# GpSimd's waits for VectorE's place in the order, left out of a gated-recurrence and maxout kernel

## Chip, cores and metric

The kernel runs on one core of a Trainium2 chip. The metric is the device time of one execution in microseconds; where a kernel was run several times, the median is given. A profiled execution is a run of its own with its own time, and the span in its profile goes from the first to the last instruction.

The engines are named as the profile names them: PE is TensorE (matmuls; PEld its weight loads), DVE is VectorE, ACT is ScalarE, POOL is GpSimd, SP is SyncE, which here issues all DMAs.

## What is computed

The inputs q, k, v and alpha have the shape batch 4, heads 8, sequence 768, head size 48. A gated linear recurrence keeps a 48x48 state for each batch and head, and its output goes as a token-by-feature matrix x (3072 x 384) through a maxout layer of two branches of width 1024:

```
for t in range(S):
    state = alpha[:, :, t, :, None] * state + einsum('bhd,bhe->bhde', k[:, :, t], v[:, :, t])
    y[:, :, t] = einsum('bhd,bhde->bhe', q[:, :, t], state)
x = y.transpose(0, 2, 1, 3).reshape(B * S, H * D)
out = maximum(x @ w1, x @ w2) @ w_out
```

## The kernel before

The sequence of each batch is cut into three blocks of 256 positions, which gives twelve blocks, n = 0 to 11. In a block, each of the 128 partitions holds two neighbouring positions, and the block is handled as two halves of 128 positions (64 partitions each). The recurrence in a block is written as matrix products: a masked product of scaled q and k within a half, and a carried state from one half to the next. The output of a block is cast into a transposed x (`xT`), and twelve groups g of two chunks of 128 tokens each run the maxout layer on it: with wd = w1 - w2, the layer is max(x@wd, 0) @ w_out + x @ (w2 @ w_out), so that one ReLU and one extra matrix m = w2 @ w_out do the work of the maximum.

Each piece of work is a named step. The steps of block n that matter here, with their line in the profile and the engines that they may run on:

- lda, ldk, ldq, ldv: loads of the block's inputs (SP, L448). ln, inv, en, ep, gg: logarithm of alpha and the exponentials (ACT).
- su{n} (L596, DVE or POOL): sum of the two positions' log alpha, both inputs in SBUF. cs{n} (L605, L610, PE): the running sums of it, by a matmul.
- ka{n} (L624) and qi{n} (L629), DVE or POOL: k and q scaled in place by the neighbour's alpha or its inverse. kt{n} (L661, DVE or POOL) and qt{n} (L666, DVE only, one input in PSUM): k and q scaled by the exponentials.
- tk, tq (L692, PE): transposes of the two; ck, cq (L490 on DVE, L488 on ACT): their copies out of PSUM. From block 8 on dk and dq (L732) do this by a DMA transpose instead.
- sc{n} (L832, PE) and pt{n} (L840, DVE, one input in PSUM): the masked product. vc{n}: cast of v. kv{n} (L752, PE): the block's own contribution to the state.
- g{n} (L765, POOL): a product of decays. With m = 2n or 2n+1 for the half, t32.m (L799) and T{m}.0, T{m}.1 (L787), on DVE or POOL: the carried state w{m-1} (L810, L812, DVE) scaled by the decay, once for the next state and twice, for the two head parities, as a matmul operand. yf{n} and y{n} (L877, PE): the block's output.
- xe (casts into xT: L488 on ACT, L490 on DVE), h{g} (L943, PE), r{g} (ReLU: L953 on ACT, L951 on DVE), o{g} (L976, PE), ev (eviction), st (store).
- at the start mask, pads, wtp, wtc, wd, woc, mp, mc prepare constants and weights, and 43 filler matmuls (L419) on a zero tile run on PE.

The number after a dot is the head half in blocks 0 and 1 (su0.0, su0.1), the head parity for T, and a part otherwise.

The order is not found at run time. `ORDER` is a string of words such as `su8.0:D`, step and engine (P PE, A ACT, D DVE, G POOL, S SP; a digit is a PSUM bank). `run()` returns the steps in that order and the loop at the end of the kernel emits them one by one; each engine then works through its own instructions in this order. Waits between engines follow from the tiles that a step reads and writes, and are added as the instructions are traced.

A step that is built with `port=True` is one that is marked as reading two inputs from SBUF, or as a copy within SBUF. The planner that once made the order (it does nothing while ORDER is there) did not start a POOL step while such a DVE step was under way, nor such a DVE step while POOL was at work. The loop carries a part of that into the program: after a marked step on DVE, the next step on POOL gets a wait for the end of that DVE step, whether or not it uses its data. There are 88 POOL steps in ORDER, and 22 of them get such a wait.

Of the kernel before, what the change touches and what calls it, by code (L numbers as in the profile page):

```python
# [299 lines left out]
def kernel(  # L300
# [15 lines left out]
    nc = tc.nc  # L316
# [687 lines left out]
        group(g, c0, nch)  # L1004
        c0 += nch

    traced = nc.cur_bb.bb.instructions
    ahead = None
    for o in plan.run():
        n = len(traced)  # L1010
        o.emit(o.eng)
        if o.eng == "DVE" and o.port:
            ahead = traced[-1]
        elif o.eng == "POOL" and ahead is not None:
            tc.add_manual_dep(traced[n], ahead.name,
                              mybir.DependencyInfo(mybir.DependencyClass.Sync, mybir.DependencyReason.DATA), reason="port")
            ahead = None
    Plan.last = plan


# [28 lines left out]
```

## Time and profile before

| | |
|---|---|
| median of 3 runs | 140.74 us (139.82 to 141.19) |
| the profiled execution's own time | 140.24 us |
| its span | 138.5 us |
| PE busy | 131.3 us, 95% of the span |
| DVE busy | 96.0 us, 69% |
| ACT busy | 79.8 us, 58% |
| POOL busy | 65.4 us, 47% |
| granted TensorE clock | 0.999 |

In lists of waits a line has the engine, the tile and line of the waiter, an arrow to the one that released it, and then the total time in us, how often, and the longest. In timelines a line has the start in us from the start of the span, the duration in us, the engine, the line of the kernel, the operation, and the tiles and shapes, output before input; x2 means two such instructions in a row, taken together. A duration in a timeline begins where the hardware records the start of an instruction, which can be before it gets to its data; waiting for a semaphore is not in it.

By its timeline POOL works on the steps of the first blocks until 21 us, pauses until 28 us, and then runs with gaps of up to 3 us until 111 us; a last T comes at 120 us.

### The profile page before, as it was taken

To read this page: it belongs to the slowest core of one execution; us is meant where nothing else is said; L and a number is where in the kernel's file an instruction comes from. 1 tells how busy PE (TensorE), PEld (TensorE's weight loads), DVE (VectorE), ACT (ScalarE), POOL (GpSimd) and SP (SyncE) were. 2 spreads that over 40 slices of the span, in tenths; PEclk is the share of its full clock that TensorE was granted. 3 is DMA by queue.
4 is the path that set the end of the run, shared out by engine and by line. 5 is a ranking of instruction groups with operands and counts; after the bars stand their busy time and mean duration, and the time that the engine had idled before them with its cause. 6 is when DMAs were issued, how large, how long until landed. Compare 5 with 4: busy or idle time off the path is not lost.

```text
span 138.5 us, 5457 instructions
## 1 busy us (share of the span) xinstructions
PE 131.3 (95%) x2348; PEld 94.0 (68%) x2348; DVE 96.0 (69%) x163; ACT 79.8 (58%) x163; POOL 65.4 (47%) x110
## 2 busy tenths in 40 slices
PE   6977999989999999999999999999999999999991
PEld 2445676655877686688866886776767876777770
DVE  5226769889877886798589759878975575685210
ACT  3526582869596779396883587543847732323320
POOL 6547360067568881796429499832625300100000
PEclk9999999999999999999999999999999999999999
DMA  4999999999999999999999991958998999541043
GB/s 108 266 304 304 380 385 326 217 249 273 267 248 226 275 262 255 282 271 278 253 274 303 280 282 29 139 98 175 287 168 215 140 199 162 193 172 60 0 170 114
DMA packets 64680, 30.76 MB, mean 222 GB/s; under 512 B 58896, under 2 KB 63120, under 8 KB 64656
## 3 DMA queue, kind: packets, MB, share of 16 engines
q1 hardware_dynamic: 64656, 30.41, 90.5%
q8 instruction: 18, 0.29, 1.0%
q14 instruction: 6, 0.05, 0.1%
HBM read 23.59 MB, written 4.72 MB: 204 GB/s over the span
## 4 chain that ended last, share of the span: by engine, by line
PE 70%; DMA 9%; SPq 9%; DVE 5%; POOL 2%; issue 2%; ACT 0%; DVEq 0%
PE PS L976 30%; PE PS L943 20%; DMA ldf<-in_k_dram 9%; PE PS L877 9%; SPq L448 6%; PE PS L832 4%; PE PS L692 4%; PE PS L752 2%; POOL ldf L629 2%; SPq L470 2%; DVE qkt L666 2%; SPq L467 1%; DVE qkt L661 1%; PE PS L605 1%; DVE pt L840 1%
## 5 line engine op out<-in xcount | busy, mean ns | idle before, releaser
L976 PE MATMUL PS<-wo,g 128*128 128x384 f16 (+1 forms) x200 | 37.6, 320 | 0.3 <-issue 0.3
L943 PE MATMUL PS<-xT,wd 128*128 128x256 f16 x288 | 36.2, 272 | 0.5 <-DVE xT L490 0.3
L840 DVE TENSOR_TENSOR pt<-PS,mask 128x1024 f16<-128x1024 f32 x24 | 28.9, 1218 | 4.2 <-PE PS L832 4.0
L943 PEld LDWEIGHTS <-wd 128*128 128x128 f16 x288 | 27.3, 98 | 5.8 <-issue 0.8
L953 ACT ACTIVATE g<-PS 128x512 f16<-128x512 f32 x34 | 19.6, 597 | 14.1 <-PE PS L943 13.9
L976 PEld LDWEIGHTS <-g 128*128 128x128 f16 x200 | 18.6, 98 | 11.2 <-issue 0.5
L629 POOL TENSOR_TENSOR ldf<-ldf,inv 128x384 f32<-128x384 f32 (+1 forms) x12 | 11.2, 933 | 17.5 <-DVE ldf L629 7.3
L488 ACT CAST xT<-PS 128x384 f16<-128x384 f32 x16 | 9.1, 595 | 15.1 <-PE PS L877 15.0
L976 PE MATMUL PS<-m,xT 128*128 128x384 f16 (+1 forms) x75 | 15.9, 320 | 0.0
L951 DVE TENSOR_SCALAR g<-PS 128x512 f16<-128x512 f32 x14 | 9.4, 684 | 7.2 <-PE PS L943 7.2
L419 PE MATMUL PS<-fz 128*128 128x512 f16 x43 | 12.9, 433 | 1.2 <-DVE fz L416 1.2
L666 DVE TENSOR_TENSOR qkt<-ldf,PS 128x768 f16<-128x768 f32 (+1 forms) x14 | 11.7, 835 | 3.2 <-POOL ldf L629 2.8
L787 POOL TENSOR_TENSOR T<-w,gg 48x192 f16<-48x192 f32 x15 | 7.8, 518 | 12.3 <-DVE T L787 3.2
L488 ACT COPY outs<-PS 128x384 f32<-128x384 f32 (+1 forms) x17 | 7.8, 460 | 9.0 <-PE PS L976 8.8
L661 POOL TENSOR_TENSOR qkt<-ldf,en 128x768 f16<-128x768 f32 (+1 forms) x7 | 11.9, 1702 | 2.0 <-ACT PS L644 1.8
L624 POOL TENSOR_TENSOR ldf<-ldf 128x384 f32<-128x384 f32 (+1 forms) x11 | 10.5, 962 | 3.4 <-DMA ldf<-in_k_dram 2.6
L588 ACT ACTIVATE loga<-ldf 128x768 f16<-128x768 f32 (+1 forms) x14 | 10.5, 751 | 2.3 <-DMA ldf<-in_alpha_dram 2.2
L787 POOL TENSOR_TENSOR T<-w,g 48x192 f16<-48x192 f32 x11 | 5.5, 503 | 12.7 <-DVE T L787 11.3
L692 PE MATMUL PS<-ident,qkt 128*128 128x128 f16 x128 | 10.3, 219 | 1.1 <-DVE qkt L666 0.9
L877 PE MATMUL PS<-pt,v 64*64 64x128 f16 x576 | 10.7, 218 | 0.0
L692 PEld LDWEIGHTS <-qkt 128*128 128x128 f16 x128 | 8.2, 98 | 3.1 <-DVE qkt L666 1.7
L490 DVE COPY qk<-PS 128x1024 f16<-128x1024 f16 (+1 forms) x12 | 7.2, 599 | 4.3 <-PE PS L692 4.1
(78 smaller groups left out, 187.4 us busy)
## 6 DMA issues: line engine op xcount, KB each, us to landing
ldf<-in_k_dram SPq DMA_DIRECT2D x12, 384.0 KB, 6.1
ldf<-in_q_dram SPq DMA_DIRECT2D x12, 384.0 KB, 6.3
ldf<-in_v_dram SPq DMA_DIRECT2D x12, 384.0 KB, 6.5
out_dram<-outs SPq DMA_DIRECT2D x23, 192.0 KB, 4.0
ldf<-in_alpha_dram SPq DMA_DIRECT2D x10, 384.0 KB, 6.0
ldf<-in_moe_w_dram SPq DMA_DIRECT2D x4, 768.0 KB, 8.2
ldf<-in_moe_w_out_dram SPq DMA_DIRECT2D x2, 768.0 KB, 9.7
ldf<-in_alpha_dram SPq DMA_DIRECT2D x4, 192.0 KB, 3.7
```

The lines of the kernel that those rows point to most:

```text
L419: plan.add(f"fill{i}", {"PE": 0.21}, lambda eng: nc.tensor.matmul(bank(fb), lhsT=fz[:, 0:128], rhs=fz, start=True, stop=True, skip_group_c ...
L488: nc.scalar.copy(out=out, in_=in_)
L629: e.tensor_mul(out=qq, in0=qq, in1=A["inv", n][:, hd])
L661: e.tensor_mul(out=hjd(qkts[i3], 1)[:, hd], in0=A["ld", n, "k"][:, hd].rearrange("p h (j d) -> p h j d", j=2), in1=f.unsqueeze(2).to_broad ...
L666: nc.vector.tensor_mul(out=hjd(qkts[i3], 0)[:, hd], in0=A["ld", n, "q"][:, hd].rearrange("p h (j d) -> p h j d", j=2), in1=f.unsqueeze(2). ...
L692: nc.tensor.transpose(t[:, a, r, j, :], src[:, j, r, :], ident16)
L787: e.tensor_mul(out=T16s[m % 4][o : o + 48, :, 48 * u : 48 * u + 48], in0=w_[o : o + 48], in1=g_[o : o + 48])
L840: nc.vector.tensor_mul(out=t.rearrange("p u r c -> p (u r) c"), in0=A["sc", n, hf].rearrange("p u (r c) -> p (u r) c", r=2), in1=mask.rear ...
L877: nc.tensor.matmul(dst, lhsT=lhsT, rhs=rhs, start=(x, u) not in begun, stop=done and ends[x, u] == i, skip_group_check=True)
L943: nc.tensor.matmul(t[:, i], lhsT=wd16[:, s, (f + i) * 128 : (f + i + 1) * 128], rhs=xT[:, s, a0 : a0 + W], start=(s == 0), stop=(s == 2), ...
L953: nc.scalar.activation(out=o, in_=i, func=ACTF.Relu)
L976: nc.tensor.matmul(A["op", t0, c], lhsT=lhsT, rhs=rhs, start=(part == 0 and j == 0), stop=(part == 1 and j + 1 == len(todo[1])))
```

## The change

After the change the loop emits the steps of `plan.run()` and does nothing else. The 22 waits that it had added are gone; the waits that follow from the tiles are still made. The steps, their engines, their order and their PSUM banks are the same, and each of the five engines has the same instructions in the same order as before. Where one of the added waits had also covered a wait for data on an earlier DVE or ACT step, that wait now stands by itself.

```
     for o in plan.run():
-        n = len(traced)
         o.emit(o.eng)
-        if o.eng == "DVE" and o.port:
-            ahead = traced[-1]
-        elif o.eng == "POOL" and ahead is not None:
-            tc.add_manual_dep(traced[n], ahead.name,
-                              mybir.DependencyInfo(mybir.DependencyClass.Sync, mybir.DependencyReason.DATA), reason="port")
-            ahead = None
     Plan.last = plan
```

The waits of these pairs go (POOL step after DVE step): su0.0 after su0.1, kt0.0 after ka0.0, qi0.0 after kt0.1, T1.0 after T1.1, g1 after woc0.1, qi1.1 after qi1.0, ka2.0 after su3.0, qi2.0 after kt2.0, qi3.0 after kt3.0, ka4.0 after su4.0, T9.0 after T9.1, ka6.0 after su5.0, T13.0 after t32.13, T10.1 after qi5.0, T11.0 after T10.0, qi9.0 after T15.0, ka8.0 after su8.0, T16.0 after T17.1, g10 after T19.0, t32.21 after su11.0, qi11.0 after kt11.0, T22.0 after T23.0.

More of the change, by code (lines that the diff above doesn't have):

```diff
@@ L1005 @@
         c0 += nch
-    traced = nc.cur_bb.bb.instructions
-    ahead = None
     for o in plan.run():
-        n = len(traced)
         o.emit(o.eng)
-        if o.eng == "DVE" and o.port:
-            ahead = traced[-1]
-        elif o.eng == "POOL" and ahead is not None:
-            tc.add_manual_dep(traced[n], ahead.name,
-                              mybir.DependencyInfo(mybir.DependencyClass.Sync, mybir.DependencyReason.DATA), reason="port")
-            ahead = None
     Plan.last = plan
```

## Prediction

> **What bounds the kernel now.** I read the busy shares first, then the waits of TensorE (PE), then those of GpSimd (POOL), and last the timelines of the places that the change touches. The page's first part:
>
> ```profile
> span 138.5 us, 5457 instructions
> PE 131.3 (95%) x2348; PEld 94.0 (68%) x2348; DVE 96.0 (69%) x163; ACT 79.8 (58%) x163; POOL 65.4 (47%) x110
> ```
>
> PE is busy 131.3 of 138.5 us, in an order that the change leaves alone. What PE still waits for is this, in full (engine, waiter, releaser: total us, times, longest):
>
> ```profile
> PE PS L419 <- DVE fz L416: 1.2, 1, 1.2
> PE PS L692 <- DVE qkt L666: 0.9, 2, 0.7
> PE PS L507 <- DMA ldf<-in_moe_w_dram: 0.7, 1, 0.7
> PE PS L943 <- DVE xT L490: 0.3, 1, 0.3
> ```
>
> Four smaller waits of 0.2 to 0.3 us follow. None names POOL. In PE's timeline the waits that are left after 13 us are some 1.3 us together: about 0.2 at 29.26 (tq1.1 for qt1.1), 0.2 at 30.23 (sc1.0 for cq1.1), 0.1 at 41.4 (kv2) and under 0.3 each at 47.9, 50.1 and 54.6. So PE's own work is the bound, and the change acts only through a wait of PE that it shortens or makes. POOL's waits are long but feed nothing late:
>
> ```profile
> POOL T L787 <- DVE T L787: 14.5, 3, 9.1
> POOL ldf L629 <- DVE ldf L629: 7.3, 1, 7.3
> POOL ldf L629 <- DVE qkt L661: 3.7, 2, 2.5
> POOL t L799 <- DVE s L596: 2.6, 1, 2.6
> ```
>
> Most of that idle time is the waits that go: the 9.1 us is T22.0 behind T23.0, the 7.3 us qi1.1 behind qi1.0.
>
> [...] Here T16.0 on DVE (second line) starts while POOL reads for qi8.0 (first line), and takes 1.04 us where its like take 0.34; in the third line it is POOL's g5 that stands behind a 0.99 us kt5.0 on DVE, 0.91 us for a step of 0.21:
>
> ```profile
> 92.63 1.11 POOL L629 TENSOR_TENSOR ldf<-ldf,inv 128x384 f32<-128x384 f32 x1
> 92.91 1.04 DVE L787 TENSOR_TENSOR T<-w,g 48x192 f16<-48x192 f32 x1
> ...
> 64.71 0.91 POOL L765 TENSOR_TENSOR g<-gg 112x4 f32<-112x4 f32 x1
> ```
>
> DVE steps with one input in PSUM (pt L840, qt L666, w L812) are not touched: 1.21 us at 83.78 beside a POOL kt. A blocked DVE step goes on some 0.14 us ahead of POOL's recorded end: T16.0 ends at 93.95, 0.34 after 93.61, POOL at 93.74. [...] qi9.0 is recorded from 79.50 and takes 1.31 us instead of 1.00, though the DVE sum that holds it up (su8.0, 0.34 us) is recorded only from 79.62. So with starts within about 0.1 us of each other, the record doesn't say who gets the interface.
>
> **The change, part by part.** The loop adds 22 edges. Two forbid nothing new (kt0.0 after ka0.0 is a data dependence; T11.0 after T10.0 is covered by the later wait for w11). Of the other 20, four were not what POOL waited for: qi0.0 and ka2.0 wait for loads, T13.0 and ka8.0 for POOL's own step before. No instruction goes, is added or moves in its queue; SP's issues keep theirs. The saved wait itself costs POOL about 0.1 us from release to start (28.15 to 28.23), all of it beside PE work. What counts is where each POOL step lands.
>
> - su0.0 (5.28): could start at 4.78 when mask is done, and pushes su0.1 from 4.87 to about 5.2. DVE next waits 1.3 us for a load, PE has filler matmuls: 0.
> - T1.0 (16.99): free at 16.40 after w0 (16.30). T1.1 on DVE, at 16.49, either holds it off, or is held until about 16.77, so 0.28 us late, and with it pt0.1 and y0, which PE starts at 18.15 right as pt0.1 ends (18.10). PE loses 0 to 0.28; the 0.2 us wait at 29.26 takes up 0.2 of it. I take +0.05.
> - g1, t32.2 (20.12, 20.41): run up to 0.4 us earlier, w2 needs them at 30.35: 0.
> - qi1.1 (28.23): both it and qi1.0 wait for the q load, seen on DVE at 27.79. POOL has started 0.13 us behind a landing (10.71 to 10.84 for qi0.0), so at about 27.9, when DVE already reads. DVE first: qt1.1 up to 0.05 us earlier, −0.05. POOL first: qi1.0 0.5 us late, qt1.0 and qt1.1 (0.55 us each) behind it, and PE's wait at 29.26 grows by 0.5, of which 0.1 is given back at 38 to 41. Range −0.05 to +0.4; I take −0.05, since DVE is ahead by 0.1.
> - qi2.0 (35.76), qi3.0 (39.43): kt2.0 and kt3.0 on DVE have begun at 34.73 and 38.01, so they keep the interface; qi2.0 gains under 0.2, qi3.0 0.5, and vc2.0 behind it 0.3. The wait of kv2 for vc2.0 at 41.4 goes: −0.1. Next late there is sc3.0's and y2's chain, which this doesn't move.
> - ka4.0 (44.27): its load lands about 43.66, start 43.8. su4.0 on DVE (43.72) should by then be some 0.3 us earlier too, with t32.4 and w4. If not, it is held 0.9 us and cs4.0 (PE 44.98) waits 0.1. I take 0, up to +0.25.
> - T9.0 (55.81) and ka6.0 (58.03): T9.0, t32.9, qi6.0 move up by about 1 us; ka6.0 starts with its load at 57.1, just ahead of su5.0 (57.16), which is held until 57.96 and ends at 58.3 instead of 57.95. DVE has 0.84 us idle ahead of its next step (58.79), and cs5.0 is due at 60.64: 0. kt6.0 gains 0.7, with 0.7 us to spare already: 0.
> - T10.1: behind qi5.0 on DVE anyway, −0.2 for itself, nobody waits: 0.
> - qi9.0 and ka8.0 (79.50, 80.79): qi9.0 can start at 77.85, ka8.0 at 78.8, next to three DVE steps with two SBUF inputs. This is the one tight place (first three lines DVE, the last two PE):
>
> ```profile
> 78.81 0.36 DVE L799 TENSOR_TENSOR t<-w,gg 112x192 f32<-112x192 f32 x1
> 79.08 0.34 DVE L787 TENSOR_TENSOR T<-w,gg 48x192 f16<-48x192 f32 x1
> 79.62 0.34 DVE L596 TENSOR_TENSOR s<-loga 128x384 f16<-128x384 f16 x1
> 80.69 0.61 PE L692 MATMUL PS<-ident,qkt 128*128 128x128 f16 x8
> 81.13 0.33 PE L605 MATMUL PS<-s,cmat 128*128 128x384 f16 x1
> ```
>
> If ka8.0 comes between t32.15 and T15.0, the latter is held from 79.08 to 79.9 and su8.0 ends at about 80.85, 0.3 us ahead of cs8.0 (81.13): 0. If it gets in ahead of t32.15, and T15.1 and ka9.0 get in ahead of T15.0 and su8.0 in their turn, su8.0 ends at about 81.85 and PE waits 0.7. I take +0.15, for the first is likelier (qi9.0 lost just such a tie to su8.0). The dk9 and dk8 transposes behind kt9.0 and kt8.0 issue some 0.7 us earlier, and land earlier; sc9 needs them only at 95.8: 0.
> - T16.0 (95.91): moves to 93.8, holds T17.0 by about 0.25; T17.1 then ends at about 96.1, and pt9.1 starts at 96.21 on PE's word: 0.
> - g10, t32.21, T21.0, ka11.0 (102.2 to 106): 1.2 us earlier; su11.0 0.2 late (0.9 at worst). cs11.0 on PE is due at 106.02 (su11.0 ends at 104.92), xe16 has 0.86 us: 0, at worst +0.2.
> - qi11.0 (109.45): free at 108.1; takes the interface ahead of kt11.0 (108.42), which then ends at 110.1 instead of 109.4. Its transpose has been issued at 109.44 and kv11 runs at 118.5: over 1 us to spare even through SP's queue (dk11, then ldv11, st4.1, dq11): 0.
> - T22.0: 9 us earlier, for yf11 at 122: 0.
>
> Sum: 0.05 − 0.05 − 0.1 + 0.15 = about +0.05 us, with bounds of −0.2 and 0.28 − 0.2 + 0.4 + 0.25 + 0.7 + 0.2 = +1.6. The profiled execution took 140.24 us around a span of 138.5, within the 139.82 to 141.19 of the runs; against their median 140.74 the sum gives 140.8. DVE is held for some 3 us in all by these hand steps, and I have followed each only to its next idle; I add 0.1 for what I don't see: 140.9.
>
> **The rivals.**
> - Forecast: DVE's delays die in its own idle time, PE keeps its pace: 140.9, 140.4 to 141.6. For it: DVE is 69% busy and waits for PE over 20 us in all.
> - The read interface taken by the slower engine. POOL's 1.0 us steps get in ahead of DVE's 0.35 us ones, one after the other, and PE waits. Its place is 78.8 to 81.1, its price 0.7 us there, and it decides from the point where su8.0 ends over 1.17 us later than now (79.96 to 81.13). With the same order at 27.8 (+0.4), 16.4 (+0.1), 43.8 (+0.25) and 104.5 (+0.2), 1.6 us: 142.3, slower. For it: T16.0's 1.04 us. Against: half a dozen ties have to fall to POOL.
> - A gain: POOL's earlier results shorten the waits of PE that are left. At most those after 26 us that hang on POOL's steps go, 0.2 + 0.2 + 0.1: 140.2. Against it: two of them end with DVE's own steps.
> - The change doesn't do what it says: POOL stands at the interface where it stood at the semaphore, and nothing moves: 140.7. So it is for qi2.0, qi3.0 and T10.1, not for the other dozen.
>
> **How the numbers follow.** Forecast 0.58, interface 0.27, gain 0.07, nothing moves 0.08. About 1% (1.4 us) is what a measurement of this kernel can tell from no change. Slower by more than that: four fifths of the interface case and a little of the forecast's tail, 0.24. Faster by more: 0.03, as PE's waits hardly add up to it. The rest, 0.73, is within 1%. The range, 140.2 to 142.4, takes in the gain and the interface case at its sum.
>
> **What would show it.** After the change, POOL's waits for DVE at L787, L629 and L799 are mostly gone, with POOL's busy time up where it is held. Held DVE steps show as T, s or qkt (L661) lines of 0.6 to 1.3 us: su5.0 near 57, T17.0 near 94, kt11.0 near 108. If I am right PE's waits stay at some 1.3 us after 13 us and PE's busy time at 131. If su8.0 ends after 81.1 and PE waits for DVE s L596, the second case has come true. Wrong altogether I would be if DVE's delays summed up over stages, so that PE waited for pt or xT as a rule.

## The result and the profile after

| | before | after |
|---|---|---|
| median of 20 runs each | 140.19 us | 140.69 us |
| ratio after / before | | 1.0054, 95% interval 1.0032 to 1.0077 |
| span of the profiled execution | 138.5 us | 139.2 us |
| PE busy | 131.3 us | 130.9 us |
| DVE busy | 96.0 us | 101.4 us |
| POOL busy | 65.4 us | 67.9 us |

The changed kernel is slower by half a per cent: 0.76 us by the ratio, 0.50 us by the medians. The medians are of all executions, while a ratio and its interval leave out those that took over 1.5% longer than the fastest of the same kernel, here 4 of the 20 of after. The same kernel was measured twice more: 1.0068 (1.0040 to 1.0097), and 1.0165 (1.0083 to 1.0248), which rests on four of six executions. All three intervals lie above 1.

The first part of the page of the kernel after shows where the time was moved, though not where it was lost. PE's busy time is what it was. DVE, with the same 163 instructions, is busy 5.4 us longer. Ten of its steps take over 0.1 us longer than before, 6.3 us together, su5.0 takes 0.44 us less, and the rest are within 0.1 us each. All eleven have two inputs in SBUF:

```profile
span 139.2 us, 5454 instructions
PE 130.9 (94%) x2348; PEld 93.7 (67%) x2348; DVE 101.4 (73%) x163; ACT 80.2 (58%) x163; POOL 67.9 (49%) x110
```

POOL's waits after the change (engine, waiter, releaser: total us, times, longest). The waits for DVE at L787 and L629, 9.1 and 7.3 us long before, are gone, and POOL now waits for loads and for data:

```profile
POOL ldf L629 <- DMA ldf<-in_q_dram: 14.1, 6, 7.8
POOL T L787 <- DVE w L812: 6.0, 3, 4.0
```

PE's waits after the change. Besides the wait for the first weights (L507, 1.1 us for 0.7), four are not in the list of before with such a size:

```profile
PE PS L976 <- issue: 0.5, 1, 0.5
PE PS L877 <- DVE pt L840: 0.4, 1, 0.4
PE PS L605 <- DVE s L596: 0.3, 1, 0.3
PE PS L877 <- issue: 0.3, 1, 0.3
```

To see what each is worth I set every matmul of after beside the same matmul of before and followed the difference of their starts. It changes in a few steps only:

| at (us, before) | PE's step | change of PE's lag | lag after it |
|---|---|---|---|
| 9.2 and 12.1 | first loads and what follows them | +0.05, −0.07 | −0.02 |
| 18.15 | y0, behind pt0.1 | +0.32 | +0.30 |
| 25.8 and 29.5 | given back at w2's transform and tq1.1 | −0.36 | −0.06 |
| 29.8 to 34.8 | kv1 and a y1 step | +0.10, −0.10 | −0.06 |
| 38.0 | h matmuls | −0.21 | −0.27 |
| 41.5 | kv2 | −0.26 | −0.53 |
| 54.87 | o matmuls, "issue" | +0.31 | −0.22 |
| 80.69 | tk7, releaser not named by the profile | +0.15 | −0.07 |
| 81.13 | cs8.0, waiting for su8.0 | +0.50 | +0.43 |
| 104.73 | y matmuls, "issue" | +0.33 | +0.76 |

So at 50 us the change was ahead by half a microsecond. It then lost that and 0.76 us more: 0.65 us around cs8.0, and 0.64 us at two places where PE waited for no tile at all. ("Issue" in the profile is time in which an engine waited for nothing that the profile shows.)

The place that the prediction called the tight one looks like this in the timelines of after (start, duration; four DVE steps, then POOL's, then PE's):

```profile
78.60 1.11 DVE L799 TENSOR_TENSOR t<-w,gg 112x192 f32<-112x192 f32 x1
79.64 0.66 DVE L787 TENSOR_TENSOR T<-w,gg 48x192 f16<-48x192 f32 x1
80.23 0.34 DVE L812 TENSOR_TENSOR w<-PS,t 112x192 f32<-112x192 f32 x1
80.50 1.02 DVE L596 TENSOR_TENSOR s<-loga 128x384 f16<-128x384 f16 x1
...
78.51 0.99 POOL L624 TENSOR_TENSOR ldf<-ldf 128x384 f32<-128x384 f32 x1
79.58 0.52 POOL L787 TENSOR_TENSOR T<-w,gg 48x192 f16<-48x192 f32 x1
80.17 1.13 POOL L624 TENSOR_TENSOR ldf<-ldf 128x384 f32<-128x384 f32 x1
...
80.62 0.61 PE L692 MATMUL PS<-ident,qkt 128*128 128x128 f16 x8
81.57 0.34 PE L605 MATMUL PS<-s,cmat 128*128 128x384 f16 x1 [0.34 <-DVE s L596]
```

Read it pair by pair. ka8.0 on POOL starts 0.09 us ahead of t32.15 on DVE, and t32.15 takes 1.11 us instead of 0.36. T15.1 starts 0.06 us ahead of T15.0: 0.66 instead of 0.34. The w step in between has an input in PSUM and takes its usual 0.34. ka9.0 starts ahead of su8.0: 1.02 instead of 0.34. POOL was first each time, twice by less than a tenth of a microsecond. su8.0 ends at 81.52 instead of 79.96, and PE, which has nothing else queued ahead of cs8.0, stands for 0.34 us.

By "held" this document means such a longer duration beside a step of the other engine, measured against the same step in before or in another trace here. POOL is held too: qi2.0, which starts at 34.90 in after while kt2.0 runs on DVE, takes 1.59 us instead of 1.01. The prediction calls what the two engines compete for the read interface. That is its name for these durations; what stands behind them in the chip is not seen in a trace.

### The profile page after: what moved, and what is told of

Read it like the earlier page. It is cut to its first block, busy times and chain, and to the rows that moved or that the text cites. A ratio compares the mean times of both kernels' runs of the same rounds, so it can differ in the third digit from the quotient of the medians.

```text
span 139.2 us, 5454 instructions
## 1 busy us (share of the span) xinstructions
PE 130.9 (94%) x2348; PEld 93.7 (67%) x2348; DVE 101.4 (73%) x163; ACT 80.2 (58%) x163; POOL 67.9 (49%) x110
## 4 chain that ended last, share of the span: by engine, by line
PE 72%; SPq 10%; DMA 9%; DVE 5%; issue 2%; ACT 0%; DVEq 0%
PE PS L976 31%; PE PS L943 19%; PE PS L877 10%; DMA ldf<-in_q_dram 9%; SPq L448 7%; PE PS L692 4%; PE PS L832 4%; SPq L470 2%; PE PS L752 2%; PE PS L605 2%; SPq L467 1%; DVE pt L840 1%; DVE t L799 1%; DVE xT L490 1%; DVE qkt L666 1%
## 5 line engine op out<-in xcount | busy, mean ns | idle before, releaser
L976 PE MATMUL PS<-wo,g 128*128 128x384 f16 (+1 forms) x200 | 37.7, 320 | 0.5 <-issue 0.5
L943 PE MATMUL PS<-xT,wd 128*128 128x256 f16 x288 | 36.0, 273 | 0.4 <-DVE xT L490 0.3
L943 PEld LDWEIGHTS <-wd 128*128 128x128 f16 x288 | 27.3, 98 | 5.7 <-issue 0.6
L976 PEld LDWEIGHTS <-g 128*128 128x128 f16 x200 | 18.6, 98 | 11.6 <-issue 0.9
L629 POOL TENSOR_TENSOR ldf<-ldf,inv 128x384 f32<-128x384 f32 (+1 forms) x12 | 11.8, 986 | 14.9 <-DMA ldf<-in_q_dram 14.1
L976 PE MATMUL PS<-m,xT 128*128 128x384 f16 (+1 forms) x75 | 15.9, 320 | 0.0
L787 POOL TENSOR_TENSOR T<-w,gg 48x192 f16<-48x192 f32 x15 | 8.1, 542 | 12.5 <-DVE w L812 5.8
L624 POOL TENSOR_TENSOR ldf<-ldf 128x384 f32<-128x384 f32 (+1 forms) x11 | 10.8, 982 | 6.0 <-DMA ldf<-in_k_dram 5.8
L877 PE MATMUL PS<-pt,v 64*64 64x128 f16 x576 | 10.7, 218 | 0.3 <-issue 0.3
L877 PEld LDWEIGHTS <-v 64*64 64x64 f16 x576 | 8.6, 107 | 2.2 <-issue 1.8
L812 DVE TENSOR_TENSOR w<-PS,t 112x192 f32<-112x192 f32 x16 | 5.6, 350 | 5.8 <-PE PS L752 5.4
```

The source lines that it names most:

```text
L624: e.tensor_mul(out=kk, in0=kk, in1=A["ld", n, "a"][:, hd, D : 2 * D])
L629: e.tensor_mul(out=qq, in0=qq, in1=A["inv", n][:, hd])
L877: nc.tensor.matmul(dst, lhsT=lhsT, rhs=rhs, start=(x, u) not in begun, stop=done and ends[x, u] == i, skip_group_check=True)
L943: nc.tensor.matmul(t[:, i], lhsT=wd16[:, s, (f + i) * 128 : (f + i + 1) * 128], rhs=xT[:, s, a0 : a0 + W], start=(s == 0), stop=(s == 2), ...
L976: nc.tensor.matmul(A["op", t0, c], lhsT=lhsT, rhs=rhs, start=(part == 0 and j == 0), stop=(part == 1 and j + 1 == len(todo[1])))
```

## The experiments

The loop is the same in the variants below; a list says which of the 22 waits are left out. With all 22 names in it, it would be the changed kernel.

```
+    FREE = (...)
...
     for o in plan.run():
...
-            tc.add_manual_dep(traced[n], ahead.name,
-                              mybir.DependencyInfo(mybir.DependencyClass.Sync, mybir.DependencyReason.DATA), reason="port")
+            if o.name not in FREE:
+                tc.add_manual_dep(traced[n], ahead.name,
+                                  mybir.DependencyInfo(mybir.DependencyClass.Sync, mybir.DependencyReason.DATA), reason="port")
             ahead = None
```

The theory to be tested was that the loss is the one at cs8.0, made by the waits of qi9.0 and ka8.0 alone. The rivals were that many small holds of DVE add up, and that the difference is luck: when loads land, and how long PE's "issue" waits are.

### The changed kernel again, and the two waits apart

The kernel after, unchanged:

> The changed kernel once more, to see which of the differences between the two traces come back. If they are made by the order of the steps, they come back to the hundredth: T1.1 held (0.67 us), su4.0 held (1.37), T9.1 held (1.36), t32.15, T15.0 and su8.0 held (1.11, 0.66, 1.02), su11.0 held (1.51), and TensorE 0.5 us later from cs8.0 on. If TensorE's two waits on nothing shown (0.53 us near 54.6, 0.31 us near 105.5) belong to the change they come back too; if they are chance, they differ by 0.1 us or more. Ratio to before 1.003 to 1.008.

All waits left out but the two:

```
+    FREE = ('su0.0', 'kt0.0', 'qi0.0', 'T1.0', 'g1', 'qi1.1', 'ka2.0', 'qi2.0', 'qi3.0', 'ka4.0', 'T9.0', 'ka6.0', 'T13.0', 'T10.1', 'T11.0', 'T16.0', 'g10', 't32.21', 'qi11.0', 'T22.0')
```

> All added waits gone but two, qi9.0 after T15.0 and ka8.0 after su8.0. Theory (the loss is made at 78.6 to 81.6 us, where GpSimd's 1 us steps hold VectorE's sums): t32.15, T15.0 and su8.0 take 0.35 us each again, cs8.0 is reached without a wait, and 0.65 us come back: ratio 1.000 or a little under, at most 1.002. Rival (the loss is spread, or comes from TensorE's waits on nothing shown): at most 0.2 us come back, ratio 1.004 or more.

Only the two left out:

```
+    FREE = ('qi9.0', 'ka8.0')
```

> The kernel before with only these two waits taken out, qi9.0 after T15.0 and ka8.0 after su8.0. Theory: TensorE waits 0.3 to 0.7 us before cs8.0 and all of it reaches the end: ratio 1.003 to 1.005. Rival (VectorE's slack takes it, the loss comes from elsewhere): ratio 0.999 to 1.001.

Measured: the changed kernel again 1.0165, above the range expected; two kept 1.0000 (0.9967 to 1.0034); two free 1.0055 (1.0027 to 1.0083). Leaving out these two alone costs what leaving out all 22 costs, and with them kept the loss is not seen. In the trace of the repeated changed kernel the held steps come back within 0.01 us, and PE's lag again rises by 0.16 at tk7 and by 0.50 at cs8.0. This execution, with a span of 141.3 us, is longer still. PE is 1.0 us later at 29 us, most of it by the loads up to 26 us. But 0.21 us of it is a hold that the first trace does not have: POOL's qi1.1 got in ahead of qi1.0, which took 0.75 us instead of 0.36. Then comes an "issue" wait of 1.35 us at 56.77, where the first trace had 0.53; the later one is 0.31 us again.

The third measurement (1.0068) shows how narrow some of these ties are. Its trace repeats the loss at tk7 and cs8.0 (+0.14 and +0.50), and the hold of qi1.0. At T21 it parts from the other two. First the DVE step T21.1 and POOL's T21.0 in after, then the same two in the third trace:

```profile
104.62 0.35 DVE L787 TENSOR_TENSOR T<-w,gg 48x192 f16<-48x192 f32 x1 [0.52 <-PE PS L877]
104.65 0.70 POOL L787 TENSOR_TENSOR T<-w,gg 48x192 f16<-48x192 f32 x1
```

```profile
106.01 1.71 DVE L787 TENSOR_TENSOR T<-w,gg 48x192 f16<-48x192 f32 x1 [0.52 <-PE PS L877]
106.04 0.51 POOL L787 TENSOR_TENSOR T<-w,gg 48x192 f16<-48x192 f32 x1
```

The recorded starts are 0.03 us apart both times. Once POOL's T21.0 is held (0.70 us instead of 0.51) and T21.1 takes its 0.35, once it is the other way round, and T21.1, with 1.71 us, stands through T21.0 and ka11.0. There PE's lag rises by 0.50 at cs11.0. So the holds at cs8.0 come back in every trace of the changed kernel, and those at qi1.0 and T21.1 differ from one execution to the next.

The timelines with the two waits kept (su8.0 on DVE, cs8.0 on PE):

```profile
80.05 0.34 DVE L596 TENSOR_TENSOR s<-loga 128x384 f16<-128x384 f16 x1
...
81.56 0.33 PE L605 MATMUL PS<-s,cmat 128*128 128x384 f16 x1
```

The same two and t32.15 with only these two waits left out:

```profile
79.09 1.12 DVE L799 TENSOR_TENSOR t<-w,gg 112x192 f32<-112x192 f32 x1
...
80.99 1.02 DVE L596 TENSOR_TENSOR s<-loga 128x384 f16<-128x384 f16 x1
...
82.06 0.34 PE L605 MATMUL PS<-s,cmat 128*128 128x384 f16 x1 [0.34 <-DVE s L596]
```

In the first su8.0 ends 1.17 us ahead of cs8.0, in the second cs8.0 starts as it ends, with the same 0.34 us of idle PE as in the changed kernel. In the second kernel PE's lag has the same three late steps as in after: +0.14, +0.50, and +0.33 at 104.73. In the first it has no step at tk7 or cs8.0. Its profiled execution (span 139.1 us) lost time elsewhere: 0.4 us by the first loads, 0.47 us within kv6 at 62.5 us, and 0.2 us at cs11.0. By its trace kv6 stood until a ReLU on ACT was done at 62.91, and ACT had just waited 1.65 us for a load of alpha. The theory stands as to place and sign.

### Is it POOL's reading?

That POOL's step holds DVE's is read off durations so far. In this variant of the changed kernel the three POOL steps beside su8.0, qi9.0, ka8.0 and ka9.0, are memsets of a tile that nobody reads, about as long as the steps that they stand for. They write SBUF and read nothing. So q and k of block 9 and k of block 8 stay unscaled: this part of the computation is left out.

```
                 e = nc.vector if eng == "DVE" else nc.gpsimd
+                if n in (8, 9):
+                    e.memset(scratch, 0.0)
+                    return
                 kk = A["ld", n, "k"][:, hd, 0:D]
...
                 e = nc.vector if eng == "DVE" else nc.gpsimd
+                if n == 9:
+                    e.memset(scratch, 0.0)
+                    return
```

> The changed kernel, with qi9.0, ka8.0 and ka9.0 on GpSimd put in as memsets of a scratch tile of about 1 us each, which write SBUF and read none (so q and k of blocks 8 and 9 stay unscaled by the neighbour's alpha). Theory (what holds VectorE is GpSimd's reading): t32.15 and su8.0 take 0.35 us again, T15.0 at most 0.7 beside T15.1, cs8.0 has no wait, 0.65 us come back against the changed kernel. Rival (any work of GpSimd at this time holds VectorE, or the loss is not theirs): su8.0 takes 1.0 us as before and TensorE waits at cs8.0.

Measured: 1.0008 (0.9975 to 1.0040). The timelines of the kernel with memsets, DVE first, then POOL and PE:

```profile
78.23 0.36 DVE L806 TENSOR_TENSOR t<-w,gg 112x192 f32<-112x192 f32 x1
78.51 0.34 DVE L794 TENSOR_TENSOR T<-w,gg 48x192 f16<-48x192 f32 x1
79.05 0.34 DVE L597 TENSOR_TENSOR s<-loga 128x384 f16<-128x384 f16 x1
...
78.22 1.01 POOL L625 MEMSET scratch<- 128x1088 f16 x1
79.30 0.51 POOL L794 TENSOR_TENSOR T<-w,gg 48x192 f16<-48x192 f32 x1
79.87 1.00 POOL L625 MEMSET scratch<- 128x1088 f16 x1
...
80.55 0.33 PE L606 MATMUL PS<-s,cmat 128*128 128x384 f16 x1
```

t32.15, T15.0 and su8.0 take 0.36, 0.34 and 0.34 us, and cs8.0 waits for nothing; PE's lag has no step at tk7 or cs8.0. POOL works as long as in after, and within some 0.1 us at the same places of PE's work, but DVE is through before the third memset begins. So the test rests on the first memset shown: t32.15 and T15.0 run within it, and su8.0 begins there. Beside ka8.0, which reads SBUF for 0.99 us, t32.15 took 1.11 us in after; beside a memset of 1.01 us it took 0.36. So POOL's being at work for a microsecond is not enough to hold DVE. A memset differs from ka8.0 in its operation too, so that it is the reading is my inference. It fits the other holds: the POOL steps that held DVE's here, at L596, L624, L629, L787 and L799 and the cast at L492, all have their inputs in SBUF.

### The gain that was in it

Only the waits of qi2.0 and qi3.0 left out, run twice:

```
+    FREE = ('qi2.0', 'qi3.0')
```

> The kernel before with only the waits of qi2.0 and qi3.0 taken out. Theory: qt2.0 and qt3.0 move up by 0.3 and 0.8 us, kv2 no longer waits, TensorE is 0.4 us ahead by 47 us; then its wait at 54.6 us takes back 0 to 0.3 us: ratio 0.997 to 0.999. Rival (TensorE's waits there hang on other steps, nothing is gained): ratio 0.9995 to 1.0005.

> Only the waits of qi2.0 and qi3.0 are gone, as in the run that came out at 0.9964 of the kernel before. Theory (the q scalings of blocks 2 and 3 give kv2 back 0.3 to 0.5 us of TensorE's wait at 41.5 us and hold no step of VectorE's that TensorE waits for): ratio 0.9964 again, between 0.994 and 0.999, so about 139.8 us where before is at 140.3. Rival (that gain was the luck of the instruction fetches[...] and of when the first loads land): ratio 0.999 to 1.002.

Measured: 0.9964 (0.9935 to 0.9993), then 0.9979 (0.9942 to 1.0016). Both point to a gain of 0.2 to 0.4%, which the second interval alone doesn't prove. In the changed kernel the gain at kv2 is plain. POOL's qi3.0 and vc2.0, then kv2 on PE, in the timelines of after:

```profile
38.44 1.20 POOL L629 TENSOR_TENSOR ldf<-ldf,inv 128x384 f32<-128x384 f32 x1 [0.66 <-DMA ldf<-in_q_dram]
...
39.84 0.82 POOL L492 CAST v<-ldf 128x768 f16<-128x768 f32 x1
...
40.94 0.41 PE L752 MATMUL PS<-v,qkt 64*64 64x48 f16 x16
```

Before, qi3.0 started at 39.43 and kv2 at 41.47. But in the first run without these two waits, the q load of block 3 landed 1.1 us later in the profiled execution than before (39.74 for 38.61), and kv2 waited:

```profile
40.26 1.00 POOL L629 TENSOR_TENSOR ldf<-ldf,inv 128x384 f32<-128x384 f32 x1 [2.13 <-ACT g L953]
...
42.31 0.43 PE L752 MATMUL PS<-v,qkt 64*64 64x48 f16 x16 [0.52 <-DVE qkt L666]
```

There PE's lag rises by 0.43 at kv2, and comes back by 0.33 at 50.3 and 0.43 at 54.9, where this execution had no "issue" wait. In the second run it falls by 0.17 at kv2. So the gain of these two waits is likely, its place is kv2 when the load is in time, and how much of the measured 0.3% is theirs stays open.

### The waits that hold nobody

Fourteen waits left out. Kept are those of T1.0, ka4.0, T9.0, qi9.0, ka8.0, T16.0, t32.21 and qi11.0, behind which a DVE step was held by more than 0.2 us in after. (qi1.1, whose wait is left out here, held qi1.0 in two other traces of the changed kernel.) Run twice:

```
+    FREE = ('su0.0', 'kt0.0', 'qi0.0', 'g1', 'qi1.1', 'ka2.0', 'qi2.0', 'qi3.0', 'ka6.0', 'T13.0', 'T10.1', 'T11.0', 'g10', 'T22.0')
```

> Only the waits are taken out that held no VectorE step up in the trace of the change: the waits of T1.0, ka4.0, T9.0, qi9.0, ka8.0, T16.0, t32.21 and qi11.0 stay, the other fourteen go. Theory: the gain of qi2.0 and qi3.0 (0.4 us by 47 us) without the loss at 79 to 82 us: ratio 0.996 to 0.999, TensorE never waits for su8.0. Rival (the gain is lost at TensorE's wait near 54.6 in any case): ratio 0.9995 to 1.001.

> Fourteen waits gone, eight kept, those of qi9.0 and ka8.0 among them. Theory (the gain of qi2.0 and qi3.0 is in it, the loss at cs8.0 is not; su11.0 and kt11.0 may be held but less than 0.2 us of that reaches TensorE): ratio 0.995 to 1.000, no better than the two waits alone. Rival (each wait that goes and holds no step of VectorE's adds a gain of its own): ratio 0.990 to 0.995, the fastest of all. Second rival (further held steps that were not seen cost as much as is won): ratio 1.000 to 1.006.

Measured: the first gave no ratio (a median of 142.79 from six runs, 140.21 to 143.20) and says nothing. The second gave 0.9971 (0.9929 to 1.0013), and a span of 137.8 us. Its DVE is busy 95.8 us, as before. The ratio rests on 8 of 22 executions, and the median of all 22 points the other way (141.08 us, 140.67 for before). From the two waits of qi2.0 and qi3.0 alone it can't be told apart, and its interval holds 1. A kernel that beats the one before for certain is not among these.

### The other holds: three early ones and three late ones

If the holds elsewhere die in DVE's idle time, their waits alone should cost nothing.

```
+    FREE = ('T1.0', 'ka4.0', 'T9.0')
```

> Only the waits of T1.0, ka4.0 and T9.0 are gone. Theory (T1.1 held beside T1.0 costs TensorE 0.3 us at 18.2 us, all of it given back by 29.5; su4.0 and T9.1, held by about 1 us, end in VectorE's own idle time): ratio 0.9985 to 1.0015, no wait of TensorE's for DVE s at L596. Rival (these three hold VectorE by some 2.3 us in all, and a part of it reaches TensorE for good): ratio 1.002 to 1.004.

```
+    FREE = ('T16.0', 't32.21', 'qi11.0')
```

> Only the waits of T16.0, t32.21 and qi11.0 are gone. Theory (T21.0 or ka11.0 hold su11.0, or T21.1 ahead of it, by over 1 us; it ends some 1.6 us later than before, and cs11.0 on TensorE, due at 106.02, starts 0.2 to 0.5 us late): ratio 1.0015 to 1.0035, and cs11.0 right behind the end of su11.0. Rival (cs11.0 still has its sum in time, as the prediction took it): ratio 0.999 to 1.001.

Measured: early 1.0070 (1.0045 to 1.0096), late 0.9999 (0.9970 to 1.0028). My expectation missed twice.

Late: su11.0 is held and ends at 105.90, and cs11.0 starts only at 106.24. So it had its sum in time, as the prediction took it; but PE had an "issue" wait of 0.39 us just before, at 104.95. Without it cs11.0 would have been due at 105.85 and lost some 0.1 us. From the timelines of the late variant:

```profile
104.39 1.51 DVE L596 TENSOR_TENSOR s<-loga 128x384 f16<-128x384 f16 x1
...
106.24 0.33 PE L605 MATMUL PS<-s,cmat 128*128 128x384 f16 x1
```

Early: leaving out these three waits alone loses as much as leaving out all 22. From the timelines of the early variant (su4.0 on DVE; T5.1 with T5.0, ka4.0 and vc3.0 on POOL; cs4.0 on PE):

```profile
44.12 2.14 DVE L596 TENSOR_TENSOR s<-loga 128x384 f16<-128x384 f16 x1
...
43.22 1.10 POOL L787 TENSOR_TENSOR T<-w,gg 48x192 f16<-48x192 f32 x2
44.28 0.99 POOL L624 TENSOR_TENSOR ldf<-ldf 128x384 f32<-128x384 f32 x1
45.22 0.82 POOL L492 CAST v<-ldf 128x768 f16<-128x768 f32 x1
...
46.31 0.34 PE L605 MATMUL PS<-s,cmat 128*128 128x384 f16 x1 [0.93 <-DVE s L596]
```

And the same steps in the changed kernel:

```profile
43.03 1.37 DVE L596 TENSOR_TENSOR s<-loga 128x384 f16<-128x384 f16 x1
...
43.19 0.99 POOL L624 TENSOR_TENSOR ldf<-ldf 128x384 f32<-128x384 f32 x1
44.44 0.82 POOL L492 CAST v<-ldf 128x768 f16<-128x768 f32 x1 [0.25 <-DMA ldf<-in_v_dram]
```

In the early variant T5.0, ka4.0 and vc3.0 follow each other without a gap, and su4.0 stands behind all of them: 2.14 us, 0.36 of it its own, and it goes on 0.14 us ahead of vc3.0's end at 46.04. PE loses 1.0 us at cs4.0, of which 0.34 comes back at 50.3. In the changed kernel vc3.0 waits 0.25 us for its load. So su4.0 stands behind the end of T5.0 and behind ka4.0, and ends at 44.40. All of this comes 1.1 us earlier there, 0.7 us of it earlier than before, in step with qi2.0 and qi3.0, so cs4.0 starts at 44.46 with its sum ready. The same wait left out costs 1.0 us or next to nothing, by where a load lands among POOL's steps and by what other waits are gone. What the waits are worth one by one can't simply be added up.

### Where PE waits for nothing

The "issue" waits of after come after 0.5 us at 54.65 and 0.3 us at 105.49. My guess was that they are waits for instructions: on the page the queue "q8 instruction" has 18 packets and 0.29 MB, 16 KB each. PE has some 4,700 instructions in the trace, which gives an estimate of 261 to a packet (4700 / 18), and the two such waits of before stand 256 of PE's instructions apart. If the guess is right, the place of such a wait belongs to the instruction's number and not to its work. So in the kernel before I left out eight filler matmuls in ORDER (fill5, 11, 14, 15, 16, 21, 26 and 29); of the lines, the one with two of them:

```
-cs1.0:P6 T1.1:D ... ldwo1:S fill5:P pads1:G ... w1:D fill21:P
+cs1.0:P6 T1.1:D ... ldwo1:S pads1:G ... w1:D ...
```

> The kernel before with eight of the 43 filler matmuls left out (fill5, 21, 16, 14, 29, 11, 26, 15, all between 17 and 25 us), which makes TensorE's stream of instructions shorter by 16 ahead of everything later. If TensorE's waits on nothing shown sit at fixed places of the stream (places 1450, 1706 and 3754 in the kernel before are 1280 and 2048 apart, multiples of 256), they move to eight matmuls further on in the work: from the 4th of the o steps' matmuls to about the 8th after it. If they hang on the work itself (a bank, a late input), they stay at the same matmuls.

Measured, in one execution: 140.33 us, span 138.6. "Issue" waits of the kernel before (first line, in a group of 12 matmuls) and of the kernel after (second, in a group of 36); each group begins at the wait:

```profile
50.32 1.47 PE L943 MATMUL PS<-xT,wd 128*128 128x256 f16 x12 [0.18 <-issue]
```

```profile
105.49 0.70 PE L877 MATMUL PS<-pt,v 64*64 64x128 f16 x36 [0.31 <-issue]
```

With eight fillers fewer:

```profile
51.11 0.60 PE L941 MATMUL PS<-xT,wd 128*128 128x256 f16 x4 [0.45 <-issue]
104.94 0.58 PE L875 MATMUL PS<-pt,v 64*64 64x128 f16 x28 [0.34 <-issue]
```

4 matmuls are left of the 12, and 28 of the 36: each wait has moved by eight matmuls within the work. Counted in PE's own instructions, weight loads included, such waits stand at 1473 and 1729 in the kernel before, at 1729 and 3777 with two free, and at 1473 and 3777 with fewer fillers, which is 193 beyond a multiple of 256 each time (in after, at 1730 and 3778, one more). The places are 256 and 2048 apart; the 1280 in the expectation is a slip. In nine traces (before, after, its repetition, two kept, two free, memsets, fewer fillers, early, late) I have 15 such waits of over 0.15 us with their matmuls, and all begin the same three groups of matmuls: 12 of h (L943 in after), 3 of o (L976) and 36 of y (L877), with fewer fillers eight matmuls further on. So the place goes with the instruction's number. What makes PE wait there is not shown. The packets on that queue are the only hint: in after two of them end at 53.09 and 104.20, and PE goes on at 54.65 and 105.49, 1.56 and 1.29 us later; in before two end at 48.91 and 53.37, and PE goes on at 50.32 and 54.87, 1.41 and 1.50 us later. But in before one ended at 103.34 as well, and PE came to place 3777 at 104.73, 1.39 us later, without a wait.

## Why the prediction was right or wrong

The predicted range, 140.2 to 142.4 us, holds the 140.69 measured, and the change is within 1%, as said. That the middle, 140.9, lies so near is luck: it stood on a median of three for the kernel before, 140.74, which came out at 140.19 over twenty. The forecast of the change itself, +0.15, is a fifth of the 0.76 that the ratio gives. That sum, too, holds two errors that stood against each other, and one part that wasn't foreseen.

- **The sum.** +0.05 and 0.1 for the unseen were taken, about +0.15; the span grew by 0.7, and the ratio says 0.0054 x 140.2 = 0.76.
- **su0.0, g1, t32.2.** Taken as 0. No step of PE's lag is there. Right.
- **T1.0.** Bounds 0 to 0.28, of which 0.2 comes back at 29.26. T1.1 took 0.67 us instead of 0.35; PE lost 0.32 at y0, a little over the bound, and had all of it back by 29.5. The hold came as described, and +0.05 was close enough.
- **qi1.1.** DVE was expected to be first, and it was, 27.87 to POOL's 27.92. qt1.0 and qt1.1 took 1.02 us instead of 1.16. In after that is right, but in the two other traces of the changed kernel POOL was first, qi1.0 took 0.75 and 0.76 us, and PE's lag rose by 0.21 and 0.24 at 28.87. The range (up to +0.4) held; which end of it came was a tie.
- **qi2.0 and qi3.0.** −0.1 taken, −0.26 at kv2 and −0.21 at 38.0 measured. This term was too small: "the wait of kv2 for vc2.0 goes" counted only the 0.1 us of that wait and not what qi2.0 and qi3.0 let DVE do earlier: qt2.0 and qt3.0 start 0.28 and 0.80 us earlier. The price of a wait on PE is not the whole gain when other waits of PE stand behind the same chain.
- **ka4.0.** 0 taken, up to 0.25. In after it is 0. But the bound was wrong: in the early variant, with su4.0 not earlier, it is held by 1.8 us, not 0.9, and PE loses 1.0. The bound counted ka4.0 alone, and neither the end of T5.0 ahead of it nor vc3.0 behind it.
- **T9.0, ka6.0.** su5.0 was expected to be held until 58.3. Instead T9.1 was held, 1.36 us at 54.89, and su5.0 was free (0.35 us). The chance was put on the wrong step, since T9.0 came at 53.93 and not at the 54.8 that was reckoned, and T9.1 met t32.9 (54.57) and then, without a gap, qi6.0 (55.04). The cost was 0, as said: cs5.0 on PE started at 60.44, behind a su5.0 that ended at 58.02.
- **T10.1, T22.0, qi11.0.** 0 each; T22.0 went 8.7 us earlier and kt11.0 took 1.72 us, with no trace on PE. Right.
- **qi9.0 and ka8.0.** +0.15 taken, +0.50 measured at cs8.0 itself, +0.65 with tk7. This is the step that failed, though the range held: "I take +0.15, for the first is likelier (qi9.0 lost just such a tie to su8.0)". The second of the two chains that it described came true in every particular: ka8.0 ahead of t32.15, T15.1 ahead of T15.0, ka9.0 ahead of su8.0. su8.0 ended at 81.52, past the 81.13 from which the rival decides; 0.7 was said for a su8.0 ending at 81.85. One tie in a record that doesn't say who was first was no ground for weighing the ties. And the three are not independent: POOL, once ahead, stayed ahead, as its step is what held DVE back to the next tie. Nor was the first a tie. In before, POOL's t32.14, which waits for nothing, starts 0.04 us ahead of the recorded end of T14.0 (77.29 to 77.33). An estimate on that ground puts qi9.0 at 77.75, where the prediction had 77.85, and ka8.0, by the 0.96 us from qi3.0 to g2, at 78.71: 0.10 ahead of t32.15. Measured were 0.08 to 0.10 in four traces out of four.
- **T16.0, g10, t32.21, T21.0, ka11.0.** T17.0 was held by 0.21 us behind T16.0 and cost nothing, as said. (The DVE step of 1.04 us that the prediction calls T16.0 is T16.1; T16.0 is POOL's.) su11.0 took 1.51 us, so it was held by 1.15 instead of the 0.2 that was likely and the 0.9 "at worst": it stood behind T21.0 and ka11.0 in one piece. In after it ended 0.26 us ahead of cs11.0, which the "issue" wait had put back; with the two waits kept cs11.0 was 0.2 us late, the worst case as priced. In the third trace of the changed kernel, where T21.1 was held too, it was 0.50 late: the worst case was priced too low.
- **What wasn't in the sum.** The two "issue" waits: +0.31 and +0.33 in PE's lag. The prediction said that PE's waits would stay at 1.3 us after 13 us. It counted two waits of this kind among them (50.1 and 54.6), but took them for constant. The later one is 0.3 us or more where DVE is held, in after, two free and late free, but also in fewer fillers, where nothing is held; and it is missing in the third trace of the changed kernel. Whether the change has a part in them stays open.

By the prediction's own sign (su8.0 after 81.1, PE waiting for DVE s L596), the rival "the read interface taken by the slower engine" is what happened, at its place and in its order: three DVE steps in a row held, by 0.75, 0.32 and 0.68 us. Its sum of 1.6 us needed all ties, and in after it had one whose cost stayed. The forecast's "DVE's delays die in its own idle time" holds for the other holds in after: of the 5.4 us that DVE is busy longer, PE felt y0 (given back) and cs8.0.

## What to carry to other kernels

Where the traces show steps of one engine held beside steps of another, look not only at the step that may be held but at how many steps follow without a gap on the other engine: su4.0 in the early variant stood behind three of them for 2.14 us, su11.0 in after behind two for 1.51. And the slower engine, once ahead at ka8.0 by 0.09 us, was ahead at the next two meetings too. In after the holds that cost were those whose end PE was due to use: one sum of 0.34 us, which had been ready 1.17 us ahead of its matmul, took back more than a change with 22 parts had won elsewhere. And what a wait is worth is to be measured with the other changes in place, since the early three cost 0.7% alone, and with the rest nothing that lasted.

## What the runs showed of the hardware that was not expected

- Held DVE steps did not take turns with POOL's where those followed without a gap. su4.0 stood through T5.0, ka4.0 and vc3.0 (2.14 us) and su11.0 through T21.0 and ka11.0 (1.51 us), steps that overlap by 0.04 to 0.05 us in the record; where it shows a gap of 0.07 to 0.08 us between POOL's steps, t32.15 and T15.0 got in.
- Recorded starts 0.03 us apart did not tell which engine is held: T21.1 on DVE took 0.35 us in one trace and 1.71 in another, with the same 0.03 us ahead of POOL's T21.0.
- A memset on POOL, of the same 1.0 us, held neither of the two DVE steps that ran within it (0.36 and 0.34 us).
- PE stopped at three places that are 256 and 2048 of its instructions apart, for 0.18 to 1.35 us in these timelines, and in before and after went on 1.29 to 1.56 us after the end of a 16 KB packet on the instruction queue. Of the 18 places in a trace that lie 193 beyond a multiple of 256, before and after stopped for over 0.15 us at two each (at one more in after). Why is open.
